# Multiplying zeros ahead of the first transposes of a layer-norm, attention and MLP kernel

## The chip, the cores and the metric

The kernel runs on one core of a Trainium2 chip. The metric is the device time of one execution in microseconds (us). Before the change, three runs took 1637.03, 1638.34 and 1639.03 us; their median is 1638.34 us.

## The reference

The input is x of 2048 rows by 512 columns, in f32. Each row is normalised (no scale or bias), and the normalised rows go two ways: through attention with 32 heads of width 16, and through a gate made of a small MLP with 1792 hidden units. The result is the input plus their product.

```python
def _A_ref(x, wqkv, wo):                      # H = 32, Dh = 16
    qkv = (x @ wqkv).reshape(B, S, 3, H, Dh).transpose(2, 0, 3, 1, 4)
    q, k, v = qkv[0], qkv[1], qkv[2]
    scores = jnp.einsum("bhqd,bhkd->bhqk", q, k) * (Dh ** -0.5)
    p = softmax(scores, axis=-1)
    o = jnp.einsum("bhqk,bhkd->bhqd", p, v)
    return o.transpose(0, 2, 1, 3).reshape(B, S, D) @ wo

def _B_ref(x, w1, b1, w2, b2):
    h = jnp.einsum("bsd,df->bsf", x, w1) + b1
    r = jnp.where(h > 0, h, 0)
    return jnp.einsum("bsf,fd->bsd", r * r, w2) + b2

x = A_x                                       # (1, 2048, 512)
xn = layernorm(x, axis=-1)                    # eps 1e-5
return x + _A_ref(xn, A_wqkv, A_wo) * silu(_B_ref(xn, B_w1, B_b1, B_w2, B_b2))
```

## The kernel before, in words

Most products are made from operands that are split in a high and a low part in a rounded f32 format, as three products of parts. A few, among them the product of probabilities and values (L373), the small ones of the tail (L760, L771), and the transposes (L1065), take plain f32 operands.

The work has three stages.

*The opening*, about 40 us. The 2048 rows come as 16 tiles of 128 rows. For each tile, `ln_stats` (VectorE's statistics, L1045 and L1047, and a square root on ScalarE, L1049), `ln_norm` (two small VectorE operations and the normalised rows xn on ScalarE, L1058), `ln_high` (four transposes of 128 by 128 on TensorE into one bank, L1065, and ScalarE's copy of the high part into xT, L1067) and `ln_low` (VectorE's subtraction that makes the low part, L1073) follow each other. A loop over i runs these for different tiles in one step: statistics of tile i, norm of tile i-1, transposes of tile i-2, low part of tile i-3. Between the transposes, `pump(n)` lets TensorE do the next n matmuls of the projections to keys, queries and values (L972, L1019), which read xT and the split weights wa_t (L905 on ScalarE, L906, L83 and L84 on GpSimd). The instructions of TensorE, ScalarE, VectorE and GpSimd stand in the order of the program text in this stage; the DMA queue on SP is ordered by a planner, by the times that it reckons.

*The lead*, up to about 174 us. TensorE goes on with the projections and takes turns with the score products for the row maxima (L298), which VectorE reduces (L305).

*The loop*, up to the end. Scores (L1234), exponentials (L1246), probabilities times values (L373), row maxima for later blocks, and the MLP and the output projection (L242, L210) interleave in an order written out by hand. A short tail finishes the last two blocks of queries.

The opening's loop takes tiles 0 and 1 apart, in its steps 2 and 3. `ln_high(0)` is the first thing that TensorE is given in the program. The tile b2_t, 128 by 512 in f32, holds the second bias; it is filled by a DMA (L1218) in the step g == 16 of the lead's loop.

Of the kernel before, what the change touches and what calls it, by code (L numbers as in the profile page):

```python
# [17 lines left out]
P = 128  # L18
# [15 lines left out]
NVT = 7  # L34
EVAC = (1, 6, 7, 9, 11, 14)
EVAC_LAST = (1, 3, 4, 5, 7, 9)
GAPS = (18, 19, 20, 22)
EPS = 1e-5

# [2 lines left out]
def kernel(  # L42
# [11 lines left out]
    nc = tc.nc  # L54
# [22 lines left out]
    b2_t = const.tile([P, D], F32, name="b2_t")  # L77
# [21 lines left out]
    with ExitStack() as ph:  # L99
# [20 lines left out]
        def make_ring(name, pool, numbers, width):  # L120
            rot.setdefault(name, []).extend(
                pool.tile([P, width], F32R, name=f"{name}{i}") for i in numbers
            )
# [255 lines left out]
        def evac(po, u):  # L379
# [3 lines left out]
            nc.scalar.activation(ot, po, AF.Copy)  # L383
            steps = EVAC_LAST if u > 28 else EVAC
            for n, fn in zip(steps, (evac_sums, evac_recip, evac_keep, evac_back, evac_norm, evac_store)):
# [292 lines left out]
        def wo_ask(k):  # L678

            c, tt = divmod(k % 16, 4)  # L680
            t0 = c * 512 + tt * P
            g = wos["f"].tile([P, D], F32, name="g", bufs=6)
            nc.sync.dma_start(g, g_d[t0 : t0 + P, :])
            if k < 16:
                t = wos["oc3"].tile([P, D], F32, name="xr", bufs=3)
                nc.sync.dma_start(t, xf[t0 : t0 + P, :])
            elif c < 2:
                t = wos["f"].tile([P, D], F32, name="s")
                nc.sync.dma_start(t, sp_d[t0 : t0 + P, :])
            else:  # L690
                t = tail[c, tt]
            wos[k] = g, t
# [30 lines left out]
        def wo_last(c):  # L723
            for tt in range(4):
                k = 16 + 4 * c + tt
                wo_ask(k + 2)
                if k in GAPS:
                    yield None, None
# [332 lines left out]
        def ln_high(t):  # L1061
            xn, xT = xts.pop(t), xTs[t // 4]
            pt = pm.tile([P, 512], F32, name="pm_t").rearrange("p (k n) -> p k n", n=P)
            for ko in range(KO):
                nc.tensor.transpose(pt[:, ko, :], xn[:, ko * P : (ko + 1) * P], ident)  # L1065
            sl = slice((t % 4) * P, (t % 4 + 1) * P)
            nc.scalar.activation(xT[:, 0, :, sl], pt, AF.Copy)  # L1067
            pts_[t] = pt
# [11 lines left out]
        def pump(n):  # L1080
# [15 lines left out]
                }  # L1096
            )
        )
        make_ring("qm", kp, range(3), 512)
        make_ring("ka", kp, range(2), S)  # L1100
        for t in range(2):
# [10 lines left out]
        for i in range(NT + 3):  # L1112
            if i in (2, 3):

                kos = slice(2 * i - 4, 2 * i - 2)
                if i == 2:
                    ln_norm(1)
                    ln_high(0)
                    split_w(wa_t, kos, slice(0, 2 * P), raw_m[:, kos])
                else:  # L1120
                    ln_low(0)
                    ln_high(1)
                    split_w(wa_t, kos, slice(0, 2 * P), raw_m[:, kos])
                    ln_norm(2)
                ln_stats(i)
            else:
                if i < NT:
                    ln_stats(i)
                if 0 <= i - 1 < NT:
                    ln_norm(i - 1)  # L1130
                if 0 <= i - 3 < NT:
                    ln_low(i - 3)
                if i == 4:

                    pump(4)
                if 0 <= i - 2 < NT:
                    ln_high(i - 2)
# [326 lines left out]
```

## Time and profile before

| | before |
|---|---|
| median of three runs | 1638.34 us |
| lowest and highest run | 1637.03 and 1639.03 us |
| profiled execution, span from first to last instruction | 1635.6 us |
| TensorE matmul busy, instructions | 1620.8 us (99%), 13300 |
| VectorE busy | 1356.8 us (83%) |
| ScalarE busy | 1189.9 us (73%) |
| GpSimd busy | 523.0 us (32%) |
| TensorE idle ahead of its first instruction | 6.6 us |

The profiled execution has its span as its own time, and no other time is listed for it; the runs' median lies 2.7 us above the span. In the profile, PE is TensorE's matmul and PEld its weight load, DVE is VectorE, ACT ScalarE, POOL GpSimd and SP the engine with the DMA queue. A row of a timeline gives the start in us from the span's beginning, the duration in us, the engine, the line of the kernel, the operation, what is written and read, the shapes, how many instructions are merged in the row, and in brackets the idle time of the engine ahead of it with what ended that. Ends of matmuls are modelled, so that neighbours overlap; the spacing of starts says more than the durations. A row of a group gives line, engine, operation, shapes and count, then busy time in us and the mean duration of one in ns, then idle time ahead of it.

### The profile page before, as it was taken

What the parts mean: (1) busy time and instruction counts of PE and PEld (TensorE: products, weight loads), DVE (VectorE), ACT (ScalarE), POOL (GpSimd) and SP (SyncE); (2) the same over time, 40 slices, a digit from 0 to 9 for tenths busy, and PEclk for the clock granted to TensorE, in tenths of its full rate; (3) what the DMA queues carried; (4) which work ended last, traced back from release to release, by engine and by line L of the source; (5) the groups of instructions that cost most, each with busy time, mean ns of one, the idle gap of its engine ahead of it and who ended that gap; (6) DMA issues with size and microseconds to landing.
All of it is one profiled execution on the core that took longest, in us unless ns stands there. A gap on an engine that the chain in (4) does not pass through costs nothing.

```text
span 1635.6 us, 35352 instructions
## 1 busy us (share of the span) xinstructions
PE 1620.8 (99%) x13300; PEld 923.2 (56%) x13300; DVE 1356.8 (83%) x2345; ACT 1189.9 (73%) x2351; POOL 523.0 (32%) x547
## 2 busy tenths in 40 slices
PE   8999999999999999999999999999999999999998
PEld 6777565456546655664466456645654565445543
DVE  6356888888888888888888888888888888887754
ACT  7311777777777777877777777777777777777786
POOL 6446568123112311321133112311321233125421
PEclk9999999999999999999999999999999999999999
DMA  8768655434333333434343334323532353246654
GB/s 299 193 210 276 205 171 145 125 100 124 83 95 100 109 93 81 129 87 112 79 121 89 83 90 141 101 68 88 147 98 61 88 144 81 60 130 195 193 170 155
DMA packets 164418, 209.18 MB, mean 128 GB/s; under 512 B 59928, under 2 KB 78872, under 8 KB 162712
## 3 DMA queue, kind: packets, MB, share of 16 engines
q1 hardware_dynamic: 163960, 206.40, 44.5%
q8 instruction: 105, 1.72, 0.5%
q14 instruction: 65, 0.53, 0.1%
q10 hardware_dynamic: 288, 0.52, 0.1%
HBM read 149.95 MB, written 56.61 MB: 126 GB/s over the span
## 4 chain that ended last, share of the span: by engine, by line
PE 99%; DVE 1%; DMA 0%; issue 0%; ACT 0%; POOL 0%; DVEq 0%; POOLq 0%
PE po L373 31%; PE pd_t L242 18%; PE pm_t L298 18%; PE se L1234 15%; PE pd_t L210 6%; PE pd_t L972 2%; PE po L972 2%; PE se L1019 1%; PE se L972 1%; PE pd_t L1019 1%; PE se L298 1%; PE po L1019 1%; PE pm_t L1234 1%; PE pm_t L1065 0%; PE pm_t L811 0%; DVE mx L305 0%
## 5 line engine op out<-in xcount | busy, mean ns | idle before, releaser
L305 DVE TENSOR_REDUCE mx<-pm_t 128x1 f32<-128x512 f32 x2000 | 1245.1, 684 | 167.8 <-PE pm_t L298 77.3
L1246 ACT ACTIVATE pt<-se 128x512 f32<-128x512 f32 x2002 | 1044.2, 617 | 257.6 <-PE se L1234 214.5
L298 PE MATMUL pm_t<-ka,qm 64*128 64x512 f32 x2000 | 793.7, 420 | 1.5 <-DVE mx L305 1.3
L1234 PE MATMUL se<-qe,ka 64*128 64x512 f32 x2002 | 674.0, 396 | 0.2 <-ACT pt L1246 0.2
L373 PE MATMUL po<-pt,v 128*32 128x512 f32 x4096 | 545.3, 604 | 0.0
L298 PEld LDWEIGHTS pm_t<-ka,qm 64*128 64x128 f32 x2000 | 350.1, 184 | 244.8 <-DVE mx L305 230.7
L242 PEld LDWEIGHTS pd_t<-xc,w1s 64*128 64x128 f32 x2688 | 334.0, 187 | 93.9 <-issue 88.9
L242 PE MATMUL pd_t<-xc,w1s 64*128 64x256 f32 x2688 | 380.2, 288 | 0.0
L1234 PEld LDWEIGHTS se<-qe,ka 64*128 64x128 f32 x2002 | 337.6, 184 | 20.7 <-ACT pt L1246 2.6
L242 PE MATMUL pd_t<-w2t,hT 64*128 64x512 f32 x1080 | 300.6, 410 | 0.0
L242 PEld LDWEIGHTS pd_t<-w2t,hT 64*128 64x128 f32 x1080 | 179.1, 184 | 80.5 <-issue 75.5
L529 POOL TENSOR_TENSOR r<-r 128x512 f32<-128x512 f32 x56 | 58.2, 1040 | 374.9 <-ACT r L526 374.9
L373 PEld LDWEIGHTS po<-pt,v 128*32 128x32 f32 x4096 | 81.0, 108 | 158.8 <-issue 136.4
L548 POOL TENSOR_TENSOR u<-u,b_t 128x512 f32<-128x512 f32 x16 | 20.6, 1287 | 316.3 <-ACT u L547 316.3
L411 POOL TENSOR_TENSOR ot<-ot,hl 128x512 f32<-128x512 f32 x31 | 39.8, 1284 | 204.4 <-DMA hl<-r_d 91.1
L210 PE MATMUL pd_t<-wot,oc 64*128 64x512 f32 x336 | 90.9, 406 | 0.0
L526 ACT ACTIVATE r<-pd_t,b_t 128x256 f32<-128x256 f32 x112 | 46.9, 470 | 57.1 <-PE pd_t L242 57.1
L210 PEld LDWEIGHTS pd_t<-wot,oc 64*128 64x128 f32 x336 | 58.4, 184 | 45.4 <-ACT pt L1246 14.2
L84 POOL TENSOR_TENSOR hT<-r,hT 128x512 fp32r<-128x512 f32 x56 | 72.2, 1290 | 4.7
L210 PE MATMUL pd_t<-w2t,hT 64*128 64x512 f32 x264 | 68.8, 393 | 0.0
L305 DVE TENSOR_REDUCE mx<-se 128x1 f32<-128x512 f32 x48 | 32.9, 685 | 40.0 <-PE pm_t L298 30.0
L210 PEld LDWEIGHTS pd_t<-w2t,hT 64*128 64x128 f32 x264 | 47.0, 184 | 6.0
(129 smaller groups left out, 928.5 us busy)
## 6 DMA issues: line engine op xcount, KB each, us to landing
w1s<-w_d SPq DMA_DIRECT2D x196, 256.0 KB
qm<-q_d SPq DMA_DIRECT2D x384, 32.0 KB
ka<-k_d SPq DMA_DIRECT2D x96, 128.0 KB
qe<-q_d SPq DMA_DIRECT2D x384, 32.0 KB
xn_d<-xT SPq DMA_DIRECT2D x8, 1024.0 KB
k_d<-hl SPq DMA_DIRECT2D x32, 256.0 KB
q_d<-hl SPq DMA_DIRECT2D x32, 256.0 KB
xc<-xn_d SPq DMA_DIRECT2D x16, 512.0 KB
```

The lines of the kernel that those rows point to most:

```text
L84: (lo or nc.gpsimd).tensor_tensor(dst[1], raw, dst[0].bitcast(F32), op=ALU.subtract)
L210: mm = nc.tensor.matmul(out_, lh(r), rh(r), start=first_ and lane == 0, stop=last_ and lane == 1, skip_group_check=True,)
L242: mm = nc.tensor.matmul(out_, lh(r), rh(r), start=first_ and lane == 0, stop=last_ and lane == 1, skip_group_check=True,)
L298: nc.tensor.matmul(ps, qms[u][p][64 * j : 64 * j + 64, qb * P : (qb + 1) * P], kas[qd, p][64 * j : 64 * j + 64, kc * 512 : (kc + 1) * 512] ...
L305: return nc.vector.tensor_reduce(mxs[u][:, c, kc : kc + 1], ps, axis=AX.X, op=ALU.max)
L373: nc.tensor.matmul(po[32 * j : 32 * j + 32, :], vs[qd][:, (4 * kb + j) * VW : (4 * kb + j) * VW + 32], pts[j], start=(kb == 0), stop=(kb = ...
L526: nc.scalar.activation(r[:, i], ps[:, i * CW : (i + 1) * CW], AF.Relu, bias=b1_t[:, fo : fo + 1])
L529: nc.gpsimd.tensor_tensor(r, r, r, op=ALU.mult)
L972: nc.tensor.matmul(out_[:, n0:n1], lh(slice(0, P)), rh(slice(0, P))[:, n0:n1], start=first_, stop=last_,)
L1019: nc.tensor.matmul(out_, lh(slice(0, P)), rh(slice(0, P)), start=first_, stop=last_)
L1234: nc.tensor.matmul(se, kas[qd, j // 2][b : b + 64, kb * P : (kb + 1) * P], qes[u][j // 2][b : b + 64, :], start=True, stop=True,)
L1246: return nc.scalar.activation(pts[j], se, AF.Exp, scale=0.25)
```

## The change

The first 128 columns of b2_t are set to zero by VectorE, behind its memsets of L75 and L287 and ahead of the seven of L1110. Ahead of the transposes of tile 0, TensorE multiplies this block of zeros with itself 24 times, in f32, 128 by 128 by 128, into the first quarter of the bank that the transposes of tile 0 then overwrite. Later tiles are as before, and b2_t gets its bias from the DMA as before.

```diff
+SPIN = 24
...
         def ln_high(t):
             xn, xT = xts.pop(t), xTs[t // 4]
             pt = pm.tile([P, 512], F32, name="pm_t").rearrange("p (k n) -> p k n", n=P)
+            for _ in range(0 if t else SPIN):
+                nc.tensor.matmul(pt[:, 0, :], idle, idle, start=True, stop=True)
             for ko in range(KO):
                 nc.tensor.transpose(pt[:, ko, :], xn[:, ko * P : (ko + 1) * P], ident)
...
+        idle = b2_t[:, :P]
+        nc.vector.memset(idle, 0.0)
         make_ring("qm", kp, range(3), 512)
         make_ring("ka", kp, range(2), S)
```

## The prediction

> **What bounds the kernel now.** I read the page first, then the timeline of the first 24 us, engine by engine, then the last 15 us, and at last the waits of TensorE behind 40 us.
>
> ```profile
> span 1635.6 us, 35352 instructions
> ...
> PE 1620.8 (99%) x13300; PEld 923.2 (56%) x13300; DVE 1356.8 (83%) x2345; ACT 1189.9 (73%) x2351; POOL 523.0 (32%) x547
> ...
> L373 PE MATMUL po<-pt,v 128*32 128x512 f32 x4096 | 545.3, 604 | 0.0
> ...
> L1065 PE MATMUL pm_t<-ident,xn 128*128 128x128 f32 x64 | 11.2, 309 | 6.6 <-ACT xn L1058 6.6
> ```
>
> TensorE is busy in 1620.8 of 1635.6 us, so it is the bound nearly everywhere. Of its 14.8 idle us, 6.6 lie ahead of the first transposes: that is the hole into which the change puts work. The opening reads (start, duration, engine, line, count, idle before):
>
> ```profile
> 0.81 0.06 DVE L75 MEMSET eps_t<- 128x1 f32 x1 [0.81 <-PEq L1451]
> 0.85 0.12 DVE L287 MEMSET m<- 128x32 f32 x2
> 0.95 0.42 DVE L1110 MEMSET vt<- 128x32 f32 x7
> ...
> 3.61 0.69 DVE L1045 BATCH_NORM_STATS2 stats<-xt 128x6 f32<-128x512 f32 x1 [2.23 <-DMA xt<-in_A_x_dram]
> ...
> 6.60 1.94 PE L1065 MATMUL pm_t<-ident,xn 128*128 128x128 f32 x8 [6.60 <-ACT xn L1058]
> 7.33 0.69 DVE L1045 BATCH_NORM_STATS2 stats<-xt 128x6 f32<-128x512 f32 x1 [1.25 <-DMA xt<-in_A_x_dram]
> 7.72 0.60 ACT L1067 ACTIVATE xT<-pm_t 128x512 fp32r<-128x512 f32 x1 [0.56 <-PE pm_t L1065]
> 8.06 0.18 DVE L1047 BATCH_NORM_AGGREGATE mv<-stats 128x2 f32<-128x6 f32 x1
> ...
> 8.35 0.69 DVE L1073 TENSOR_TENSOR xT<-pm_t,xT 128x512 fp32r<-128x512 f32 x1
> ...
> 9.56 0.58 PE L972 MATMUL se<-xT,wa_t 128*128 128x256 f32 x1 [1.02 <-ACT xT L1067]
> ...
> 10.30 1.01 PE L972 MATMUL se<-xT,wa_t 128*128 128x256 f32 x3 [0.16 <-POOL wa_t L906]
> ...
> 13.05 1.05 PE L1065 MATMUL pm_t<-ident,xn 128*128 128x128 f32 x4
> ...
> 13.75 1.50 PE L972 MATMUL se<-xT,wa_t 128*128 128x256 f32 x8
> ...
> 14.84 0.81 ACT L1058 ACTIVATE xn<-xt,rstd 128x512 f32<-128x512 f32 x1
> ...
> 15.09 0.60 PE L1065 MATMUL pm_t<-ident,xn 128*128 128x128 f32 x4
> ...
> 15.38 0.68 DVE L1045 BATCH_NORM_STATS2 stats<-xt 128x6 f32<-128x512 f32 x1
> ...
> 15.73 0.60 ACT L1067 ACTIVATE xT<-pm_t 128x512 fp32r<-128x512 f32 x1
> ...
> 16.48 0.60 PE L1065 MATMUL pm_t<-ident,xn 128*128 128x128 f32 x4
> ...
> 17.09 0.68 DVE L1045 BATCH_NORM_STATS2 stats<-xt 128x6 f32<-128x512 f32 x1
> ...
> 18.61 0.60 PE L1065 MATMUL pm_t<-ident,xn 128*128 128x128 f32 x4
> ...
> 20.70 0.60 PE L1065 MATMUL pm_t<-ident,xn 128*128 128x128 f32 x4
> ```
>
> Three things are in it. First, TensorE is slow at the start: four transposes take 1.05 us at 13.05 and 0.60 us at 15.09. The eight of 6.60 last 1.94 us, the last one 0.42 of it, so one starts every (1.94 - 0.42) / 7 = 0.217 us; with a late one at 0.27 (the f32 row of L771 below has 276 ns for the same size), four in 0.60 start every 0.11 us. That is half speed until some point between 13.75 and 15.09. (The page's row of granted clock prints full speed there already; the durations say otherwise and I go by them.) Second, until about 16 us the pace is VectorE's: its statistics of one tile follow another by 1.71 us (15.38, 17.09) with hardly a gap, and in its in-order queue the subtraction of tile 0 (8.35) stands ahead of all that. Third, from 16.48 on the pace is TensorE's: its transposes come at 16.48, 18.61 and 20.70, 2.1 us apart, slower than VectorE could go. The sixth tile's normalised rows (tile 5; rows 0 to 4 and their transposes come before it in the same two groups) are done at 14.84 + 0.81 = 15.65, but TensorE takes them up at 16.48, 0.83 us late.
>
> **The change, part by part.** It adds 24 matmuls and one memset, and removes nothing. What does such a matmul cost? The late part of the trace has true f32 matmuls:
>
> ```profile
> 1623.58 1.06 PE L760 MATMUL se<-sel,tot 128*128 128x4 f32 x8
> 1624.57 1.08 PE L771 MATMUL se<-ident,tsm 128*32 128x128 f32 x32
> ...
> 1629.52 0.87 PE L811 MATMUL pd_t<-w,thl 128*128 128x512 f32 x3
> ...
> L771 PE MATMUL se<-ident,tsm 128*32 128x128 f32 x32 | 1.1, 276 | 0.0
> ```
>
> Count calls against instructions. L771 is called 2 x 2 x 4 = 16 times and stands with x32; L760 4 times, x8; L373 32 x 16 x 4 = 2048 times, x4096. Each f32 matmul is two instructions. A transpose is one: 16 x 4 calls, x64. So 24 calls are 48 instructions. The length of one: L771 moves 128 columns in four column tiles side by side; 32 instructions over four tiles are 8 in a row, in about 1.0 us, 0.125 us each at full speed with what lies between. The transposes, also 128 f32 columns over the full array, give 0.11 at full speed and 0.217 at half. I take 0.107 and 0.213. The weight load that comes with each instruction lies beside the instruction before it: L760 has next to no columns to move and still goes through eight full f32 loads at (1.06 - 0.25) / 7 = 0.115 us, no longer than the moving part, and the transposes show loads and moves overlapped.
>
> When do they start? They wait for the memset of the zeros, which VectorE does behind the rows at 0.85 (end 0.97). Its 128 columns cost between one row of 32 columns, 0.06, and four, 0.24; I take 0.15. TensorE's sequencer is up at 0.81, by what released L75. So about 1.2 us. The memset pushes the seven of 0.95 back by 0.15; they end at 1.5 and VectorE has nothing to do until 3.61, so this is free. Without that gap it would be 0.15 us. Queued behind the waiting first matmul is all of TensorE's work, but none of it is ready before 6.60. The bank was free; the same engine writes it in order. The later DMA into the tile that lends the zeros is issued in the loop that begins past 60 us, long after, and waits for nothing.
>
> When do they speed up? If activity lifts the half speed, the trace bounds the time. Counted from 9.56, behind which TensorE has one short gap of 0.16, it took 13.75 - 9.56 = 4.2 to 15.09 - 9.56 = 5.5 us; counted from 6.60 it took at most 8.5, but with 1.02 us idle inside. The dense stretch is the nearer case: I take 4.8 and keep 4.2 and 8.5.
>
> At half speed 4.8 us hold 22.5 instructions; the other 25.5 take 2.73 us. The zeros end at 1.2 + 4.8 + 2.73 = 8.7, not at 6.6. So **the block is too long for its hole**: tile 0's transposes start at 8.8, 2.2 us late, but at full speed. From 15.09 to 15.73 a fast set needs 0.64 us until ScalarE's copy, the slow one 7.72 - 6.60 = 1.12. The copy of tile 0 starts at 8.8 + 0.64 = 9.44 for 7.72: 1.72 us late. VectorE's subtraction moves by as much (VectorE itself is free at 8.24), and with it the whole chain of tiles that it paces. The sixth tile is normalised at 15.65 + 1.72 = 17.37, and TensorE, fast by now, is no longer 0.83 behind: its transposes start at 17.5 for 16.48, 1.0 us late. From there TensorE's own 2.1 us a tile lead as before, VectorE's 1.71 catch up, and what is late stays late:
>
> ```profile
> PE pm_t L298 <- DVE mx L305: 1.3, 4, 0.3
> PE se L1234 <- ACT pt L1246: 0.2, 1, 0.2
> ```
>
> These are all of TensorE's waits between 40 us and 1630 us: 1.5 us. No slack in which a delay could end. The sum: 1635.6 + 1.0 = 1636.6 of span. The median of the runs lies 1638.34 - 1635.6 = 2.7 above the span, the share outside it; hence **1639.3 us**. With 4.2 for the speed-up the zeros end 0.3 earlier, +0.7; with 8.5 they end at 10.6, +2.9.
>
> [...]
>
> **The rivals.** (a) *The zeros never speed TensorE up*, since nothing in the array toggles, or because the pauses count. Every row of the trace at full speed works on live data, so this can't be excluded. 48 x 0.213 = 10.2 us end at 11.4. The transposes are then slow too: copy at 11.5 + 1.12 = 12.6, 4.9 late; 0.7 of it is regained at the sixth tile: +4.2, 1642.5 us. It decides as soon as the first transposes behind the zeros still take 1.05 us for four.
>
> (b) *Weight loads don't hide* when both halves of an f32 matmul load the same block: a pair costs load plus move, 0.43 slow and 0.21 fast. 11 instructions in the first 4.8 us, 37 at 0.213: end at 13.8; copy at 13.9 + 0.64, 6.8 late, less 0.83: +6.0, 1644.4 us. For it: no row has full-width f32 loads and moves of equal length that are no transposes. Against it: the transposes have exactly that and overlap.
>
> (c) *The block is short*: one instruction per call, or half the length. 24 x 0.213 = 5.1 at most, over by 6.3. Transposes at 6.60, fast; the copy at 7.24; but VectorE holds the subtraction until 8.24, so only 0.1 is won there. What is won is TensorE's 0.83 lateness at the sixth tile, bar 0.1: about -0.8, 1637.5 us. The counts of x4096 and x32 speak against it. This is what the change would bring if it fitted.
>
> (d) *The DMA queue is put in another order.* The stores and loads of the opening on the SP queue follow a planner's times, which 24 more matmuls move. The gain is bounded: of the 14.8 idle us 6.6 + 1.02 + 0.16 stand above and 1635.6 - (1629.52 + 0.87) = 5.2 lie behind the last matmul, so 1.8 us are left to win. A loss is open.
>
> **How the numbers follow.** About 0.2%, 3.3 us, is what a measurement of this kernel can tell from no change, so the limits are 1635.1 and 1641.6. The likeliest case (+0.7 to +2.9, and 1 us of spread between runs on both sides) has 0.66 and lies within, but for 0.02: 1637.6 to 1642.2. (a) has 0.11 and is slower, (b) 0.10 and slower, (c) 0.09 and the same, (d) 0.04, half slower and half faster. Slower 0.02 + 0.11 + 0.10 + 0.02 = 0.25, same 0.64 + 0.09 = 0.73, faster 0.02. The range takes in the likeliest, (c) and (a): 1637.2 to 1643.0; it leaves out (b), (d) and a rest.
>
> **What would show it.** The changed profile should have 48 matmuls and 48 loads of the new line from about 1.2 us on; spacing 0.213, then 0.107, with the step between 5 and 10 us; four transposes in 0.60 us from the first; the first copy of L1067 at 9 to 10 us instead of 7.72; the transposes of 16.48 about 1 us later; then the same rows with that offset up to the end. I am wrong in sign if the zeros end ahead of 7 us, and in size if VectorE's chain runs ahead of the late transposes, if loads and moves alternate, or if offsets at 20 us and at 1600 us differ by more than a microsecond.

## The result, and the profile after

The changed kernel took 1640.05 us (median of 21 runs, 1637.91 to 1641.59) beside 1637.71 us for the kernel before in the same comparison (21 runs). The ratio is 1.0012, with a 95% interval of 1.0007 to 1.0018: slower by 2.3 us in the medians, by 1.1 to 2.9 us by the interval. A second comparison gave 1639.84 beside 1637.68, ratio 1.0013 (1.0004 to 1.0021). The sign and the place are those of the forecast; the size was forecast at +1.0.

The page of the profiled execution, which took 1638.23 us, near the lower end of the 21, begins:

```profile
span 1636.5 us, 35449 instructions
...
PE 1626.5 (99%) x13348; PEld 929.6 (57%) x13348; DVE 1356.7 (83%) x2346; ACT 1189.9 (73%) x2351; POOL 522.9 (32%) x547
```

There are 48 matmuls and 48 weight loads more, as counted. The rows of its timeline that answer to those shown of before (lines behind the change are shifted: the transposes are L1068, ScalarE's copy L1070, the projections L973, the zeros L1066, the first row maxima L299):

```profile
0.94 0.17 DVE L1103 MEMSET b_t<- 128x128 f32 x1
...
1.16 7.27 PE L1066 MATMUL pm_t<-b_t 128*128 128x128 f32 x48 [1.16 <-DVE b_t L1103]
...
8.27 1.04 PE L1068 MATMUL pm_t<-ident,xn 128*128 128x128 f32 x8
8.91 0.60 ACT L1070 ACTIVATE xT<-pm_t 128x512 fp32r<-128x512 f32 x1 [1.83 <-PE pm_t L1068]
...
10.74 0.38 PE L973 MATMUL se<-xT,wa_t 128*128 128x256 f32 x1 [1.44 <-ACT xT L1070]
...
11.48 1.01 PE L973 MATMUL se<-xT,wa_t 128*128 128x256 f32 x3 [0.36 <-POOL wa_t L907]
...
12.29 1.06 PE L1068 MATMUL pm_t<-ident,xn 128*128 128x128 f32 x4
...
14.23 0.93 PE L1068 MATMUL pm_t<-ident,xn 128*128 128x128 f32 x4
...
15.94 0.60 PE L1068 MATMUL pm_t<-ident,xn 128*128 128x128 f32 x4
...
17.33 0.60 PE L1068 MATMUL pm_t<-ident,xn 128*128 128x128 f32 x4
...
61.38 0.49 PE L299 MATMUL se<-ka,qm 64*128 64x512 f32 x1
...
1630.38 0.86 PE L812 MATMUL pd_t<-w,thl 128*128 128x512 f32 x3
```

In the kernel before, the first row maximum started here, so that an offset can be read at one and the same instruction in every kernel:

```profile
60.54 0.49 PE L298 MATMUL se<-ka,qm 64*128 64x512 f32 x1
```

The zeros run from 1.16 until the transposes begin at 8.27, beyond the hole that ended at 6.60. The transposes of tile 0 start 1.67 us late and are fast (the eight of tiles 0 and 1 in 1.04 us for 1.94). Tile 5's transposes (17.33 for 16.48) are 0.85 late, the first row maximum 0.84, the last matmul 1630.38 - 1629.52 = 0.86. What the opening loses is neither made up nor added to in the 1570 us behind it.

One thing was not foreseen. The transposes of tiles 2 and 3 are slow again: 1.06 and 0.93 us for four. A table by stretches (columns: stretch, its length, busy time and count of PE, PEld, DVE, ACT and POOL, granted clock, DMA share and GB/s; the last row is the second half of the second) shows why:

```profile
0.00:4.65 4.65, 3.49 (x16) 3.49 (x17) 1.81 (x14) 1.47 (x2) 3.92 (x8) 1.00 0.61 177
4.65:11.48 6.83, 5.04 (x43) 4.61 (x41) 3.92 (x14) 4.49 (x10) 1.69 (x3) 1.00 1.03 373
11.48:14.89 3.41, 3.40 (x15) 3.14 (x16) 3.27 (x11) 3.06 (x7) 3.33 (x4) 0.50 1.05 388
14.89:20.00 5.11, 5.11 (x46) 5.11 (x45) 4.90 (x16) 4.68 (x10) 4.86 (x6) 1.00 0.59 214
...
8.06:11.48 3.42, 1.63 (x13) 1.20 (x11) 1.87 (x6) 2.57 (x6) 1.32 (x2) 1.00 1.03 386
```

Up to 4.65 us 16 of the zeros' instructions take 3.49 us, 0.218 each: half the speed of the rest, though the clock column prints 1.00 for this stretch as well. From 4.65 on, which is called the step below, the other 32 run fast: 3.62 us until the transposes at 8.27, 0.11 each as an estimate. From 11.48 to 14.89, one stretch of 3.41 us, the granted clock stands at 0.50. **The clock that the zeros lifted fell back** once TensorE had waited 1.44 and 0.36 us (the two bracketed gaps at 10.74 and 11.48). TensorE was busy for 1.63 of the 3.42 us ahead of the fall (last row). Whether the waits are the cause is tested below, with the bridge and the block of 48.

### The profile page after: what moved, and what is told of

It is laid out like the page before. It is cut to its first block, busy times and chain, and to the rows that moved or that the text cites. A ratio compares the mean times of both kernels' runs of the same rounds, so it can differ in the third digit from the quotient of the medians.

```text
span 1636.5 us, 35449 instructions
## 1 busy us (share of the span) xinstructions
PE 1626.5 (99%) x13348; PEld 929.6 (57%) x13348; DVE 1356.7 (83%) x2346; ACT 1189.9 (73%) x2351; POOL 522.9 (32%) x547
## 4 chain that ended last, share of the span: by engine, by line
PE 99%; DVE 0%; issue 0%; ACT 0%; POOL 0%; DVEq 0%; POOLq 0%; ACTq 0%
PE po L374 31%; PE pd_t L243 19%; PE pm_t L299 18%; PE se L1239 14%; PE pd_t L211 6%; PE pd_t L973 2%; PE po L973 2%; PE se L1020 1%; PE se L973 1%; PE pd_t L1020 1%; PE se L299 1%; PE po L1020 1%; PE pm_t L1239 0%; PE pm_t L1066 0%; PE pm_t L1068 0%; PE pm_t L812 0%
## 5 line engine op out<-in xcount | busy, mean ns | idle before, releaser
L299 PE MATMUL pm_t<-ka,qm 64*128 64x512 f32 x2000 | 794.3, 420 | 1.5 <-DVE mx L306 1.3
L299 PEld LDWEIGHTS pm_t<-ka,qm 64*128 64x128 f32 x2000 | 350.6, 184 | 244.9 <-DVE mx L306 230.5
```

The source lines that it names most:

```text
L299: nc.tensor.matmul(ps, qms[u][p][64 * j : 64 * j + 64, qb * P : (qb + 1) * P], kas[qd, p][64 * j : 64 * j + 64, kc * 512 : (kc + 1) * 512] ...
```

## The experiments

All experiments stand beside runs of the kernel before on the same chip, whose medians were 1637.6 to 1637.7 us. Four questions were open. Is it the length of the block that costs? Does the fall-back cost anything? Does the half of the loss that the first profile doesn't show (+0.9 there, +2.3 in the median) come from the moment of the step? And does the other order of the DMA queue matter?

**Half the block.** It ends inside the hole.

```diff
-SPIN = 24
+SPIN = 12
```

> 12 multiplications of zeros in place of 24, all else as changed. Overrun theory (the loss is what the block sticks out of the 6.6 us hole, and 24 stick out by 1.7 us or more): 24 instructions of 0.213 us end at 1.16 + 5.1 = 6.3 us even if none runs fast, so the first transposes start at 6.60 as before; they are fast in the runs in which the step of the clock falls inside the block. Time between -0.8 us and 0 against the kernel before. Queue-order theory (what is lost comes from the reordered DMA queue, not from the block): the planner's order of the SP queue is that of the kernel before here, so 0 as well, but then the first transposes of the changed kernel should not matter. Theory that any zeros ahead cost: half of +2.3 us, about +1.2.

Measured: 1638.27 us for 1637.63, ratio 1.0003 (0.9995 to 1.0012), not to be told from no change. Its timeline, and a line of its table by stretches:

```profile
1.16 5.18 PE L1066 MATMUL pm_t<-b_t 128*128 128x128 f32 x24 [1.16 <-DVE b_t L1103]
6.54 1.27 PE L1068 MATMUL pm_t<-ident,xn 128*128 128x128 f32 x8 [0.19 <-ACT xn L1059]
9.47 1.31 PE L973 MATMUL se<-xT,wa_t 128*128 128x256 f32 x4 [1.66 <-ACT xT L1070]
...
9.30:16.13 6.83, 6.41 (x27) 5.79 (x28) 6.55 (x20) 5.61 (x12) 4.95 (x6) 0.50 1.05 391
```

The zeros end at 6.34 and nothing sticks out. But the clock falls back here too, at 9.30, in a gap of 1.66 us, for two such stretches (6.83 us), to 16.13; the kernel before had fast transposes at 15.09. So there is no gain; with its first transposes on time, this profile was 0.8 us late at the first row maximum (61.35 for 60.54). Another 0.6 came at about 180 us, where TensorE, between two matmuls of the MLP, waited for a load that the kernel before never waits for:

```profile
179.57 0.39 PE L243 MATMUL pd_t<-xc,w1s 64*128 64x256 f32 x1 [0.17 <-DMA xc<-xn_d]
```

This load was issued at 173.93 us, 1.9 later than in the kernel before (172.03); what held it up is not shown.

**A bridge over the gap.** The change, and zeros where TensorE waits behind tile 1.

```diff
 SPIN = 24
+BRIDGE = 6
...
                 if i == 4:
+                    bridge = pd.tile([P, 512], F32, name="pd_t")
+                    for _ in range(BRIDGE):
+                        nc.tensor.matmul(bridge[:, :P], idle, idle, start=True, stop=True)
                     pump(4)
```

> The change, and 6 more multiplications of zeros (12 instructions, 1.3 us at full speed) between the transposes of tile 1 and the first projection, into the bank pd_t, which nobody uses yet. The profiled run of the change had TensorE idle there for 1.44 us and its clock fell back to half from 11.5 to 14.9 us. Fall-back theory: bridged, the clock stays full, the transposes of tiles 2 and 3 take 0.60 us for four instead of 1.06 and 0.93, and the kernel gains 0.3 to 0.5 us on the change, about +1.9 us against the kernel before. Overrun theory alone: VectorE paces this stretch, so nothing is gained: +2.3 us; the bridge itself fits into its gap when it runs fast.

> The bridged change once more beside the change itself. Fall-back theory: the bridged kernel is 1.0 to 2.0 us below the change in the median, as +0.6 to +2.3 in the two earlier comparisons, since without the bridge the clock falls back for at least one window of 3.4 us; no stretch at half clock behind its step. If the first comparison was chance: the two medians agree within 0.5 us.

Measured: 1638.24 for 1637.63 (1.0004, 0.9996 to 1.0013), and the second time 1638.34 for 1637.68 (1.0002, 0.9993 to 1.0011), beside the change's own 1639.84 on that chip. The bridge takes 1.5 us off the change on that chip, and 1.7 when the first series and the first series of the change are each set against the kernel before beside them. The first profile, then two rows of the second:

```profile
8.69 1.04 PE L1069 MATMUL pm_t<-ident,xn 128*128 128x128 f32 x8
9.56 1.50 PE L1142 MATMUL pd_t<-b_t 128*128 128x128 f32 x12
...
12.38 0.66 PE L1069 MATMUL pm_t<-ident,xn 128*128 128x128 f32 x4
...
61.42 0.49 PE L300 MATMUL se<-ka,qm 64*128 64x512 f32 x1
...
5.52:22.00 16.48, 15.34 (x125) 14.29 (x124) 12.76 (x39) 13.16 (x27) 10.34 (x11) 1.00 0.80 294
```

```profile
9.20 1.04 PE L1069 MATMUL pm_t<-ident,xn 128*128 128x128 f32 x8
...
61.92 0.49 PE L300 MATMUL se<-ka,qm 64*128 64x512 f32 x1
```

The clock stays at 1.00 behind its step; tile 2's transposes take 0.66 for 1.06. With the fall-back gone the prediction's own rule is left bare. It puts the later rows late by (T + 0.64 + 0.13 - 7.72) + 15.65 - 16.48, that is T - 7.8, where T is the start of tile 0's transposes. T = 8.69 gives 0.9, and 61.42 - 60.54 is 0.88; T = 9.20 gives 1.4, and 61.92 - 60.54 is 1.38.

The runs without a profile list a mean granted clock, too. One stretch of 3.41 us at half speed is about 0.001 of the span. The clock is 0.998 or lower in 16 of the 32 runs of the two series of the change, in none of the 22 of the bridged one, and in none of the 74 of the kernel before that were taken beside the experiments.

**The change again, twice**, unedited, for profiles at other moments.

> The changed kernel once more, for a profile at another moment and beside the next two on one chip. Its first profile was +0.9 us on that of the kernel before, its median +2.3. [...] Rival (the spread comes from somewhere later in the kernel): the same opening to 0.1 us, +0.85 at 17 us, and the offset grows behind that.

> A third profile of the changed kernel. [...] Rival: opening as in the first profile.

Measured: 1639.84 us in the median, 1640.12 for the profiled run; 1638.32 for the single third run. The first of the two, and then two rows of the other:

```profile
1.17 8.41 PE L1066 MATMUL pm_t<-b_t 128*128 128x128 f32 x48 [1.17 <-DVE b_t L1103]
9.41 1.04 PE L1068 MATMUL pm_t<-ident,xn 128*128 128x128 f32 x8
...
63.11 0.49 PE L299 MATMUL se<-ka,qm 64*128 64x512 f32 x1
...
1.17:7.04 5.87, 5.87 (x27) 5.87 (x28) 2.74 (x14) 2.72 (x5) 3.71 (x3) 1.00 0.89 273
7.04:13.87 6.83, 4.93 (x39) 4.19 (x37) 3.92 (x12) 3.79 (x10) 2.57 (x3) 1.00 1.04 383
13.87:17.28 3.41, 2.92 (x13) 2.92 (x14) 3.27 (x11) 3.02 (x7) 3.24 (x4) 0.50 1.05 387
```

```profile
8.48 1.04 PE L1068 MATMUL pm_t<-ident,xn 128*128 128x128 f32 x8
...
61.70 0.49 PE L299 MATMUL se<-ka,qm 64*128 64x512 f32 x1
```

The same kernel has its step at 4.65 in one run and at 7.04 in another, 2.39 later, and its transposes at 8.27 and 9.41, 1.14 later: about half, as the prediction's working has it. The clock falls back in both. The rule T - 7.8 gives 0.5, 0.7 and 1.6 for the three profiles of the change; the first row maximum is late by 0.84, 1.16 and 2.57. The rest, 0.4, 0.5 and 1.0, is put down to the fall-back: no row prices it apart, but profiles without one follow the rule to 0.05 (the two bridged ones, and the block of 48 below). At the last matmul the three are late by 0.86, 0.94 and 2.58, so in these profiles the difference does not come from somewhere later.

**Late, but quiet.** The transposes start late behind a memset on GpSimd, with one multiplication of zeros in place of 24.

```diff
-SPIN = 24
+SPIN = 1
...
-        nc.vector.memset(idle, 0.0)
...
+        nc.gpsimd.memset(rot["ka"][1][32:64, :].bitcast(F32), 1.0)
+        nc.gpsimd.memset(rot["ka"][1][32:64, :1024].bitcast(F32), 1.0)
+        nc.gpsimd.memset(idle, 0.0)
```

> One multiplication of zeros in place of 24, and it waits for a memset on GpSimd that ends at 8.0 us behind two filler memsets (on a buffer that gets its value again later): TensorE's transposes start late, at about 8.4 us, as in the profiled run of the change, but TensorE has done nothing before. Delay theory: the start is +1.8 us as with the zeros; the transposes are slow as in the kernel before; so the later rows are +1.3 to +1.9 us. If the speed-up by zeros buys something back, this kernel is slower than the change's profiled run (+0.85 us in its later rows) by about 0.5 us. If it buys nothing, it stands at +0.85 us as well.

Measured: 1639.99 us for 1637.63, ratio 1.0014 (1.0005 to 1.0023).

```profile
8.18 0.80 PE L1066 MATMUL pm_t<-b_t 128*128 128x128 f32 x2 [8.18 <-POOL b_t L1118]
8.77 1.91 PE L1068 MATMUL pm_t<-ident,xn 128*128 128x128 f32 x8
...
62.94 0.49 PE L299 MATMUL se<-ka,qm 64*128 64x512 f32 x1
```

Its transposes start 2.17 late and are slow, and the row maximum is 2.40 late. That is 1.4 more than T - 7.8 = 1.0 would be with a fast TensorE: as an estimate from this, the speed that the zeros bring is worth about 1.4 us where it lasts, and 0.4 to 1.0 less where it falls back. In the median, the change with its 48 instructions is no better than this kernel that only waits (1640.05 and 1639.84 beside 1639.99).

**Twice the block.**

```diff
-SPIN = 24
+SPIN = 48
```

> 48 multiplications of zeros in place of 24. Overrun theory: the 24 more are 48 instructions of 0.107 us at full speed, 5.1 us, all behind the hole and on the path: +5.1 us on the change, +7.4 us against the kernel before, and the first transposes at 8.3 + 5.1 = 13.4 us or later. Queue-order theory: no proportion to the number. Theory that TensorE has slack later: less than 5.1 us.

Measured: 1644.17 us for 1637.63, ratio 1.0041 (1.0028 to 1.0053), 4.1 us above the change.

```profile
14.59 1.04 PE L1068 MATMUL pm_t<-ident,xn 128*128 128x128 f32 x8
17.06 0.38 PE L973 MATMUL se<-xT,wa_t 128*128 128x256 f32 x1 [1.43 <-ACT xT L1070]
...
1636.31 0.87 PE L812 MATMUL pd_t<-w,thl 128*128 128x512 f32 x3
...
6.66:14.60 7.94, 7.94 (x73) 7.94 (x73) 0.88 (x2) 0.28 (x1) 0.00 (x0) 1.00 1.03 379
```

73 instructions in 7.94 us, 0.109 each at full speed. T = 14.59 gives 6.8 by the rule; the last matmul is 1636.31 - 1629.52 = 6.79 late. Against the change's profiles the block costs 5.2 to 6.3 more in T for 24 calls; in the median it is 4.1 and not the 5.1 forecast. That would fit a kernel that pays for no fall-back, as in this profile; of its five runs, two have a mean granted clock of 0.998, so those may have paid for one.

This profile says what the wait alone doesn't. TensorE waits 1.43 us and then 0.36 us (17.80) behind the transposes, as in the change, yet the clock stays at 1.00. In the three tables that have a fall, the steps up and down of the opening lie 3.41 us or twice that apart (4.65, 11.48 and 14.89 in the first profile of the change, 7.04, 13.87 and 17.28 in the second, 5.89, 9.30 and 16.13 with 12 zeros). As an estimate from these, the time of the other profiles is cut here into stretches of 3.41 us that start at their own step (6.66 in this one); no table shows an edge where the clock stays. Here the end of a stretch, 16.90, falls into the waits, and neither stretch holds them all; the stretch ahead of the fall in the kernel of 12 stands below for comparison:

```profile
13.48:16.90 3.42, 2.15 (x20) 1.91 (x18) 1.00 (x4) 1.67 (x4) 0.42 (x1) 1.00 1.08 370
16.90:20.31 3.41, 2.31 (x14) 1.81 (x15) 3.27 (x11) 3.04 (x7) 3.33 (x4) 1.00 0.36 44
```

```profile
5.89:9.30 3.41, 1.73 (x12) 1.10 (x11) 1.68 (x6) 2.99 (x6) 0.84 (x1) 1.00 1.03 375
```

The clock fell behind the stretches in which TensorE was busy for 1.63, 1.52 and 1.62 us (the change's three profiles, the last two added up from the rows of their timelines) and 1.73 us (12 zeros). It stayed behind those with 2.15 and 2.31 us here, and with 1.90 us in the kernel of 12 and a bridge of 6: a wait of 1.51 us in one stretch of 3.41 (4.45 to 7.86, an estimate from its rows), and fast transposes behind it.

```profile
1.16 4.50 PE L1067 MATMUL pm_t<-b_t 128*128 128x128 f32 x24 [1.16 <-DVE b_t L1104]
7.17 1.27 PE L1069 MATMUL pm_t<-ident,xn 128*128 128x128 f32 x8 [1.51 <-ACT xn L1060]
...
10.89 0.66 PE L1069 MATMUL pm_t<-ident,xn 128*128 128x128 f32 x4
```

So in these six profiles the falls went with the lower busy times, not with the longer wait: 1.43 us stands here without a fall, 1.44 us in the change with one. What makes the clock fall is not shown.

**Both remedies.** 12 ahead, and a bridge of 4 (twice) or 6.

> 12 multiplications ahead (they end at 6.3 us at half speed, inside the hole) and 4 as a bridge behind the transposes of tile 1 (0.85 us at full, 1.7 us at half speed). If both theories hold and the step falls inside the zeros, the opening is fast from 6.6 us on: -0.3 to -0.8 us against the kernel before. If the step falls later, the first transposes are slow as before and the bridge has them wait up to 0.8 us: 0 to +0.5. Median expected at -0.2 us. Overrun theory alone: 0.

> 12 multiplications ahead and a bridge of 4 once more, to see whether the 0.86 us by which its median lay below the kernel before stands. If both theories hold (nothing sticks out of the hole, the clock does not fall back): 0.6 to 1.1 us below the kernel before again. If the first was chance: within 0.3 us of it.

> 12 ahead and a bridge of 6. With the bridge of 4, TensorE still idled 0.53 us ahead of the first projection; 4 more instructions take 0.43 us at full speed. If any idle time there lets the clock fall in part of the runs, this one gains up to 0.3 us more. If 0.53 us is short enough, nothing: VectorE paces this stretch. Where the clock is still at half, 12 instructions take 2.6 us behind 8.5 us and hold the first projection back by 1.5 us: up to 0.5 us lost in such runs.

Measured: with 4, 1636.82 for 1637.68 (0.9996, 0.9987 to 1.0005), then 1637.95 for 1637.58 (1.0002, 0.9992 to 1.0011); with 6, 1637.12 for 1637.58 (0.9996, 0.9987 to 1.0005). The first profile of the bridge of 4:

```profile
7.80 1.06 PE L1142 MATMUL pd_t<-b_t 128*128 128x128 f32 x8
9.39 0.39 PE L974 MATMUL se<-xT,wa_t 128*128 128x256 f32 x1 [0.53 <-ACT xT L1071]
...
59.66 0.49 PE L300 MATMUL se<-ka,qm 64*128 64x512 f32 x1
```

Here the row maximum is 0.9 us early, as the case "the block is short" had it (-0.8). But the second series of the same kernel runs from 1635.80 to 1639.83, and its median is above the kernel before. In it the five runs with a mean granted clock of 0.999 took 1635.80 to 1637.96 us, four with 0.998 1637.78 to 1638.42, and two with 0.997 1639.76 and 1639.83; so the slow ones had a lower clock, though no profile shows where. No version here is shown to beat the kernel before.

**The DMA queue.** The planner did put the SP queue of the change in another order; compare its rows before (first fence) and after:

```profile
27.70 1.18 SPq L1028 DMA_DIRECT2D v_d<-vt  x1
28.93 1.33 SPq L1221 DMA_DIRECT2D xn_d<-xT  x1
31.49 1.70 SPq L927 DMA_DIRECT2D k_d<-hl  x2
```

```profile
30.58 1.57 SPq L138 DMA_DIRECT2D qm<-q_d  x3
32.28 1.72 SPq L928 DMA_DIRECT2D k_d<-hl  x2
```

No kernel was made for this. In the change's first profile the offset that is 0.85 at 17.33, 0.84 at 61.38 and 0.86 at 1630.38 leaves it no room; the 0.6 us that the kernel of 12 lost to a load is not explained by this and stays open.

## Why the prediction was right, and where it was short

*The count and the rate held.* Two instructions per f32 call, 0.218 us at half and 0.109 at full speed (forecast 0.213 and 0.107), weight loads hidden (73 loads beside 73 matmuls in the 7.94 us of the kernel of 48): rival (b) is out, and so is (c).

*The start held.* 1.16 us for 1.2, the memset 0.17 for 0.15; it delayed nothing.

*Zeros do lift the clock*, so rival (a) is out. The step came 3.5 us behind the start in the first profile and 3.9 and 5.9 in the others. The forecast was 4.8, with 4.2 and 8.5 as ends: two of the three lie below its lower end, and a fixed delay from the start of dense work does not hold. (The 3.9 is an estimate: by the other two, transposes at 8.48 go with a step at about 5.1.) In these profiles the place of the step moves T by up to 1.14 us.

*The delay through VectorE's chain held to 0.1 us*: late by T - 7.8, as the bridged kernels (at the first row maximum) and the block of 48 show.

*The step that failed is "TensorE, fast by now".* The forecast let it stay fast from tile 0 on. The wait of 1.4 us ahead of the first projections, which the rows of before show in its slow form (1.02 at 9.56), left TensorE busy for only 1.5 to 1.6 us of a stretch of 3.41, and the clock fell back for 3.41 us in the two profiles of the change that have a table (in the third four transposes take 1.05 and 1.03 us again, at 12.34 and 14.44). This term, put at nothing, is 0.4 to 1.0 us in the profiles, and 1.5 to 1.7 us in the medians with and without a bridge. Why the medians differ by more than the three profiles do is open; three moments don't make a distribution. The one profiled run near the median (1640.12 us) was 2.57 us late: 1.6 by the rule and 1.0 from the fall-back. The 2.3 us of the medians lie inside the 0.84 to 2.57 us of the three profiles; no run shows how the step spreads over the rest.

*Rival (d) came true in its premise* (the queue was reordered) and cost nothing in the change's first profile; no kernel tested it alone.

*That the time came so near is in part luck.* The forecast of 1639.3 us lies 0.75 below the 1640.05 measured, but the change in time, +1.0 for +2.3, is off by 1.3. The sum took the share outside the span as 2.7 us; in the profiled run of the change it is 1638.23 - 1636.5 = 1.7, and in most runs about 1.8. The 0.9 too much there hid more than half of what the forecast span was short by (1636.6 us for 1638.1 in the median run). One sum of the working is off as well: the likeliest case less 1 us of spread is 1639.0 - 1 = 1638.0 at its lower end and not 1637.6; nothing else hangs on it.

## What to carry to other kernels

Work put into a hole to lift a clock is best counted at the slow rate: here it ran at 0.218 us an instruction first, for 3.49 us in the first profile of the change, so that 24 instructions ended at 6.34 us, inside the hole of 6.60, and 48 held the transposes back to 8.27. And count what comes behind the hole: the clock that was lifted ahead of waits of 1.44 and 0.36 us was lost behind them in all three profiles of the change, and kept in the one of 48 zeros, so look at the gaps after the hole before filling the hole. A gain that hangs on where the step falls can show in one profile and not in the median, as 12 zeros with a bridge of 4 did.

## What the runs showed of the hardware

TensorE's granted clock fell to 0.50 for one stretch of 3.41 us in the first two profiles of the change (11.48 to 14.89 and 13.87 to 17.28) and for 6.83 us with 12 zeros (9.30 to 16.13), each time behind 3.41 us in which TensorE was busy for 1.52 to 1.73 us. It stayed at 1.00 in the kernel of 48 zeros behind 2.15 and 2.31 us, with a wait of 1.43 us over their edge. With the gaps bridged, three tables have it at 1.00 from the step to 22 us (bridge of 6 behind 24, twice, and bridge of 4 behind 12); in the other two bridged profiles sets of four transposes take 0.60 to 0.66 us from 10.36 and 10.89 on, as at full speed. With zeros ahead TensorE went from 0.218 us an instruction (16 in 3.49 us) to 0.109 (73 in 7.94 us with 48 zeros); that step came 3.5 to 5.9 us behind the first zero in the six profiles with a table up to it. The kernel before, without zeros, came to full speed between 13.75 and 15.09 on live data: four transposes take 1.05 us at 13.05 and 0.60 at 15.09. 24 multiplications of f32 blocks are 48 instructions (x48 in the change's profile).
